# Value-gate products with the gate weights held still on column quarters, and three turns back

## The chip, the cores and the metric

The kernel runs on one core of one Trainium2 chip. The core has TensorE (PE, matrix products; the trace shows its weight loads apart, as PEld), VectorE (DVE), ScalarE (ACT), GpSimd (POOL) and SyncE (SP, which issues most transfers). The metric is the device time of one execution in microseconds, as the median of several runs; lower is better.

## The reference, cut to what matters

Windowed attention (8 batches, 8 heads, 576 tokens, 64 columns a head, window 128) feeds a mixture of 8 experts with two experts a token.

```
scores = scale * q @ k.T + bias, masked to 0 <= rel < 128      # per batch and head
attn   = softmax(scores)
x      = (attn @ v), heads side by side                        # 4608 x 512
logits = x @ w_gate;  noise_scale = log1p(exp(x @ w_noise))    # 4608 x 8 each
noisy  = logits + noise_scale * noise
top2 of noisy per token, softmax over the two
out[t] = sum over the two experts e: weight * relu(x[t] @ w1[e]) @ w2[e]
```

The gate logits are linear in x, and x is linear in v. So the kernel multiplies v by the gate weights first, a 16-column product for each head ("value gates"), appends these 16 columns to the head's 64 value columns, and gets its share of the logits out of the same product with the attention weights that gives x.

## The kernel before, in words

Work is cut into 32 pairs (a batch and two heads) of attention, then the experts' two products. A pair has five blocks of up to 128 queries. On PE a pair is: `scores` (L578, 18 products of 64x64 stationary tiles, in two bursts of 12 and 6), `trans` (L599, 13 transposes of the softmax tiles), and `weigh` (L616, 32 products of the turned weights with the values and their gate columns). DVE takes maxima (`top`), ACT exponentials (`soft`), and either of them evacuates PSUM (`evac`, L291 on ACT and L295 on DVE).

Every second pair starts a new value tile: 16 groups of value gates in all, one for a batch and four heads (`gates_of_values`). A group takes the transposed values `vt` (128 rows: two heads of 64 columns, twice, for 576 keys). For each of five blocks of keys and each of the two halves `c`, the keys' 128 (or 64) columns are loaded as the stationary operand and the 32 gate columns of `wgn` stream through (L516): 10 products, each shown by the trace as two records of PE, since a product of 32-bit numbers is done in two passes. The result has keys on partitions, and two copies (`gates_in`) put it beside the raw values `vraw`.

PSUM has eight banks: four for scores (two rings of two), one for the low half of `weigh`, and three in the ring `tb` that transposes, value gates, the high half of `weigh` and routing share.

After each batch its tokens are routed (logits, top two, a scatter of token numbers). Feed-forward work for experts 0 and 1 on the batches that are already routed (the first wave: L1306 first product, L1366 and L1371 second product) is woven into the end of attention; the second wave does all the rest and runs to the end.

The order of instructions on each engine is fixed before the run, by a small planner in the kernel (`Order`). It gives each piece of work a rank and an assumed duration, and plays the program with queues, buffers and transfers. The ranks come from a table of constants (`LOAD`, `STAGE`, `FFN0`, `HOLD` and others); `TURNED` is the assumed duration of a group of value gates on PE.

Of the kernel before, what the change touches and what calls it, by code (L numbers as in the profile page):

```python
# [8 lines left out]
F32 = mybir.dt.float32  # L9
# [10 lines left out]
B, H, S, D = 8, 8, 576, 64  # L20
N, DM, E, F = B * S, H * D, 8, 1024
W = 128
NQ = 5
# [18 lines left out]
BLOCKS = tuple(((DONE[-1], c - DONE[-1]),) if e < EARLY else ((0, 512), (512, 384), (896, c - 896)) for e, c in enumerate(CAPS))  # L42
HELD, MORE = 16, 8
LISTS = ((0, EARLY, DONE[-1], (CAP - DONE[-1] + 127) // 128), (EARLY, E, 0, (CAP + 127) // 128))
ZERO = 1340.8
LOAD = 885.97
VALUES = 252.36
GATE = (105.31, -144.49)
GATES = 473.91
ROUTE = -23.25  # L50
SCATTER = (-321.47, -1089.37, 1184.84)
FFN0, FFN1 = 144.02, 197.25
WEIGHTS = ((71.95, 139.15), (422.16, -43.96))
SEQUENCE = ((0, 0), (0, 1), (1, 0), (1, 1), (0, 2), (1, 2), (0, 3), (1, 3))
TOKENS = -282.53
STAGE = (793.51, 96.25, -887.0, -336.08, -38.4, -877.89, 219.3, -111.42)
MIDDLE = 339.64
RESULT = -1110.7
WEIGHTS_LATE = 521.8
SOON = -136.65  # L60
LISTED = (-1113.58, -714.36)
BIG, PARTS = 1899.33, 796.08
TIGHT = (1, 5, 7)
LATE = (-1193.61, -724.08, 210.07, 80.21, -368.28, 29.29, 453.02, -305.32, -534.88, -183.12, 1321.79, 251.28, 666.5, 311.48)
LAG = 0.2
SP_COST = 0.55
DMA_RATE = 360e3
DMA_LAG = 4.0
REST = 0.74
PACE = (36.32, -15.48)  # L70
HOLD = (-53.94, 64.86)
AHEAD = 301.5
GATHER_LAG, SCATTER_LAG, LISTED_LAG, TURN_LAG = 4.4, 5.0, 3.0, 4.0
STAY, TURN = -236.48, 0.13
TICK, WARM = 3.413, 1.28
WEIGH, TURNED = 2.2, 1.1

# [35 lines left out]
class Order:  # L115
# [48 lines left out]
    def put(self, ring, tile_):  # L164
        ring.free.append(tile_)
        self.serve(ring)
# [85 lines left out]
def attention_moe(ctx: ExitStack, tc: tile.TileContext, qk_, v, vt_, w_gate, w_noise, noise, w12,  # L252
                  out, xs, slots, eye):
    nc = tc.nc
# [10 lines left out]
    ap_ = att.enter_context(tc.tile_pool(name="att", bufs=1))  # L265
    order = Order()
    spawn, put, mark = order.spawn, order.put, order.set

    def ring(pool, count, shape, dtype, name):
        return Ring([pool.tile(shape, dtype, name=f"{name}{i}") for i in range(count)])  # L270

    def pe(us, rank, emit, join=True, shape=0):
        return Op((("PE", us, rank),), emit, join, shape)
# [10 lines left out]
    def either(a, b, rank, late, emit):  # L284
        return Op((("ACT", a, rank), ("DVE", b, rank + late)), emit)
# [3 lines left out]
    def copy(e, o, i, **kw):  # L289
        if e == "ACT":  # L290
            nc.scalar.activation(o, i, AF.Copy, **kw)  # L291
        elif kw:
            nc.vector.tensor_scalar(o, i, kw["scale"], None, op0=OP.mult)
        else:
            nc.vector.tensor_copy(o, i)  # L295
# [12 lines left out]
    denr = ring(ap_, 2, [128, 2, NQ, 2], F32, "den")  # L308
    xr = ring(ap_, 3, [128, NQ, 256], F32, "x")
    ltr = ring(ap_, 2, [128, NQ, H, 16], F32, "lt")  # L310
    gsr = ring(ap_, 1, [128, 128], F32, "gs")

    PAIRS = B * NP
    n = PAIRS * NQ
# [10 lines left out]
    ident = const.tile([128, 128], F32, name="ident")  # L325
# [7 lines left out]
    wgn = const.tile([128, 4, 32], F32, name="wgn")  # L333
# [25 lines left out]
    def masks():  # L359
# [10 lines left out]
        for g in range(NP):  # L370
            for h, odd in ((2 * g, 0), (2 * g + 1, 0), (2 * g, 1), (2 * g + 1, 1)):
                yield either(0.28, 0.17, -20 + 5 * g, LATE[9], lambda e, h=h, odd=odd: bias_of(e, h, odd))
            if not g:
# [4 lines left out]
    def set_ups():  # L378
# [41 lines left out]
        for z, (ap, r) in enumerate([(xs, N * XW)] + [(out, r * DM) for r in range(0, NPAD, 512)]):  # L420
            row_ = 4 * DM + (0 if z else rest_)
            yield from move(1e6, 16 + ZERO * z, lambda ap=ap, r=r, row_=row_: nc.sync.dma_start(
                dram(ap, r, [[row_, 128], [DM, 4], [1, DM]]), zero[:, None, :].to_broadcast([128, 4, DM])))
# [12 lines left out]
    def gate_weight(z, w, h, parts):  # L436
        yield from move(2e4, -LOAD + GATES, lambda: nc.sync.dma_start(
            wgn[h * D:h * D + D, :, h * 16 + z * E:h * 16 + z * E + E],
# [5 lines left out]
    sb, tb, ob, yb = Ring([bank[0:2], bank[5:7]]), Ring([*bank[2:4], bank[7]]), Ring([bank[4]]), Ring([])  # L444
# [9 lines left out]
    def loads():  # L454

        for k in range(PAIRS):
            rank = 5 * k - LOAD
            t = qks[k] = yield (qkr, rank)
# [17 lines left out]
    def all_values():  # L476
        for y in range(2 * B):
            rank = 10 * y - VALUES
            u = yield (vtr, rank)
# [22 lines left out]
    def gates_of_values(y, t, u, turned, landed):  # L502

        rank = 10 * y + GATE[0]
        spawn(ones_of(y, t, landed, rank))
        yield gated
        yield turned
        a = yield (tb, rank)
        c0 = y % 2 * 2

        def products():
            for i in range(NQ):
                r = min(S - 128 * i, 128)
                for c in range(2):
                    o = 64 * i + 32 * c
                    nc.tensor.matmul(a[0:r, o:o + 32], u[:, c, 128 * i:128 * i + r], wgn[:, c0 + c],  # L516
                                     start=i == c == 0, stop=False, skip_group_check=True)

        yield pe(TURNED, rank, products)
        put(vtr, u)  # L520
        yield landed
        done = Event(2)
        for z in range(2):
            spawn(gates_in(y, t, a, z, rank, done))
        yield done
        put(tb, a)

    def gates_in(y, t, a, z, rank, done):
        if z:
            to, from_ = t[0:64, 4, :, D:D + 16], a[0:64, 256:320].rearrange("p (h e) -> p h e", h=4)  # L530
        else:
            to, from_ = t[:, 0:4, :, D:D + 16], a[:, 0:256].rearrange("p (i h e) -> p i h e", i=4, h=4)
        yield either(*((0.11, 0.13) if z else (0.28, 0.34)), rank, LATE[2], lambda e: copy(e, to, from_))
        mark(done)
        mark(valued[y])
# [116 lines left out]
    def burst(k, group):  # L652
        r0 = k * NQ + group[0] + STAGE[0]
        if not k:
# [16 lines left out]
    def unit(k, i, group, s, topped):  # L671
        t = k * NQ + i
        r0, r1, r2, r3, r4, r5, r6, r7 = (t + z for z in STAGE)
        g, y = k % NP, k // 2
# [69 lines left out]
    def part(i, a, pt, r4, parted):  # L744

        half_ = i in (0, 4)
        yield either(0.28 if half_ else 0.39, 0.34 if half_ else 0.47, r4, LATE[3], lambda e: evac(e, i, a, pt))
        put(tb, a)
# [24 lines left out]
    def logits(b):  # L773


        yield written[b]
        rank = 20 * b + GATE[1]
        lt = lts[b]
# [18 lines left out]
    u = ap_.tile([128, NQ, E], F32, name="u")  # L797
# [16 lines left out]
    def route(b):  # L814
        yield gates[b]
        if b:
            yield routed[b - 1]
        rank = 20 * b - ROUTE
        V = nc.vector
# [155 lines left out]
        else:  # L975
            yield Op((("POOL", 1.55, rank), ("DVE", 0.8, rank + LATE[10])), lambda g: tables(engine[g], 2), slows=0.4)
        a = yield (tb, rank)
# [8 lines left out]

        rank = 20 * b + SCATTER[2 if b == B - 1 else b + 1 in CUTS]
        yield pool(1.08, rank, scatter)
# [148 lines left out]
    def early_rank(e, f):  # L1137
        return WEIGHTS[e][0] + WEIGHTS[e][1] * f if e < EARLY else 1000 + step_of(e) + f

# [23 lines left out]
    def weight(e, f, t, rank):  # L1163
# [18 lines left out]
        if e < EARLY:  # L1182
            yield either(1.35, 1.13, rank, LATE[12], largest)
        else:
# [23 lines left out]
    def split(e, f, z, t, parts, rank, both):  # L1208
# [11 lines left out]
        if e < EARLY:  # L1220
            yield Op((("POOL", 2.85, rank), ("DVE", 0.66, rank + WEIGHTS_LATE)), low, slows=0.6)
        else:
# [115 lines left out]
    def middle(blk, f, t, rank, end):  # L1338
# [11 lines left out]
        else:  # L1350
# [3 lines left out]
            blk.h[f][1].append(hl)  # L1354
        yield either(0.052 + c * 0.000833, 0.067 + c * 0.00104, rank - MIDDLE, LATE[8], lambda e: relu(
            e, hh[:, 0:c], t[:, 0:c]))
        yield dve(0.07 + c * 0.00104, rank - MIDDLE, lambda: nc.vector.scalar_tensor_tensor(  # L1357
            hl[:, 0:c], t[:, 0:c], 0.0, hh[:, 0:c], op0=OP.max, op1=OP.subtract))
# [24 lines left out]
    def downs_of(steps, ranks):  # L1383
        for (blk, f), rank in zip(steps, ranks):
# [24 lines left out]
            for piece in pieces_:  # L1409
                end = yield pe(0.655 * len(piece) + (0.1 if blk.cut is not None else 0.0), rank,  # L1410
                               lambda: [mm2(blk, f, j, r, ev[2]) for j, r in piece], False)
                if f == 7:
                    for j, r in piece:
                        spawn(result(blk, j, r, rank - RESULT, end))
            spawn(after(blk, f, ev[3] if blk.last else None, end))

    def last_downs(blk, rank):

        blk.y = []
        for j, r in blk.tiles:  # L1420
# [4 lines left out]
            for f in range(8):  # L1425
# [3 lines left out]
                end = yield pe(0.655, rank, lambda: mm2(blk, f, j, r, ev[2]), False)  # L1429
            spawn(result(blk, j, r, rank - RESULT, end))  # L1430
        to = yield (yor, rank)
# [95 lines left out]
    def first_tokens():  # L1527
        for e, blk in enumerate(first):
            yield from tokens(blk, ranks1[8 * e] - TOKENS)

# [84 lines left out]
    def second_ids():  # L1615
        yield order.now + LISTED_LAG
        for (e0, e1, s0, nt), (rows, t) in zip(LISTS, ids2):
            if e0:
                yield ranked
            rank = LISTED[e0 > 0]  # L1620
            yield from token_numbers(range(e0, e1), s0, nt, rows, t, rank)
# [22 lines left out]
    def second_tokens():  # L1644
        for q, blk in enumerate(second):
            yield from tokens(blk, 1000 + 8 * q - AHEAD if q else FFN1 - SOON)

# [32 lines left out]
    with ExitStack() as ob:  # L1680
# [4 lines left out]
        with tc.For_i(0, reach, 1) as j:  # L1685
            e = nc.values_load(tab[:, 0, bass.ds(j, 1)], engines=[mybir.EngineType.SP], min_val=0, max_val=E - 1)
            r = nc.values_load(tab[:, 1, bass.ds(j, 1)], engines=[mybir.EngineType.SP], min_val=0,
                               max_val=(E * EROWS - 128) // UNIT)
# [11 lines left out]
            t = op.tile([128, 4, 128], F32, name="ot")  # L1700
# [5 lines left out]
            for a in range(2):  # L1706
                h = op.tile([128, 4, 128], F32, name="oh")
# [10 lines left out]
            o = ow.tile([128, DM], F32, name="oo")  # L1718
# [47 lines left out]
```

## Time and profile before

| what | value |
|---|---|
| median of 3 runs | 1049.65 us (1047.02 to 1052.15) |
| the profiled execution: time | 1048.76 us |
| its span, first to last instruction | 1046.9 us |
| PE busy | 1022.2 us (98% of the span) |
| PE records of the value gates (L516) | 320, in 16 groups, from 16.4 to 224.4 us |
| mean granted TensorE clock | 0.995 |

The span lies 1.9 us under the execution's time, and that time 0.9 us under the median. Busy times of PE come from records that overlap: a record is longer than the time until the next one starts, so what a piece of work costs is read from start to start.

### The profile page before, as it was taken

To read this page: it belongs to the slowest core of one execution; us is meant where nothing else is said; L and a number is where in the kernel's file an instruction comes from. 1 tells how busy PE (TensorE), PEld (TensorE's weight loads), DVE (VectorE), ACT (ScalarE), POOL (GpSimd) and SP (SyncE) were. 2 spreads that over 40 slices of the span, in tenths; PEclk is the share of its full clock that TensorE was granted. 3 is DMA by queue.
4 is the path that set the end of the run, shared out by engine and by line. 5 is a ranking of instruction groups with operands and counts; after the bars stand their busy time and mean duration, and the time that the engine had idled before them with its cause. 6 is when DMAs were issued, how large, how long until landed. Compare 5 with 4: busy or idle time off the path is not lost.

```text
span 1046.9 us, 23487 instructions
## 1 busy us (share of the span) xinstructions
PE 1022.2 (98%) x8934; PEld 666.1 (64%) x8934; DVE 616.2 (59%) x2350; ACT 471.1 (45%) x1118; POOL 348.4 (33%) x458
## 2 busy tenths in 40 slices
PE   7999999999999999999999999999999999999997
PEld 6787778886666679654565457545744664564455
DVE  5988988977779981469836733663457241332111
ACT  5878776764422662225633433362326231332211
POOL 1085798124433531320433033312332330421103
PEclk9999999999999999999999999999999999999999
DMA  8989898963357971793768167805953471753113
GB/s 297 404 278 372 305 298 302 293 201 66 64 106 196 192 135 24 198 265 66 102 86 212 48 112 117 215 12 100 197 132 45 87 98 36 123 72 48 15 26 50
DMA packets 137123, 157.00 MB, mean 150 GB/s; under 512 B 90529, under 2 KB 100849, under 8 KB 137009
## 3 DMA queue, kind: packets, MB, share of 16 engines
q1 hardware_dynamic: 119488, 116.14, 39.4%
q0 software_dynamic: 17520, 39.34, 22.0%
q8 instruction: 71, 1.16, 0.5%
q14 instruction: 44, 0.35, 0.1%
HBM read 95.11 MB, written 40.91 MB: 130 GB/s over the span
## 4 chain that ended last, share of the span: by engine, by line
PE 90%; DVE 5%; ACT 2%; DMA 1%; issue 1%; POOL 1%; SPq 0%; DVEq 0%; ACTq 0%
PE bank L1306 35%; PE bank L1366 29%; PE bank L1371 6%; PE bank L616 6%; PE bank L599 5%; PE bank L578 4%; PE bank L516 3%; DVE held L1218 1%; PE bank L1479 1%; DVE p L584 1%; ACT pT L291 1%; PE bank L1447 1%; DVE ahl L1357 0%; POOL out_dram L1501 0%; DMA xs_dram<-x 0%
## 5 line engine op out<-in xcount | busy, mean ns | idle before, releaser
L1306 PEld LDWEIGHTS <-held 128*128 128x128 f16 x2424 | 234.2, 98 | 127.3 <-issue 2.9
L1306 PE MATMUL bank<-bx,held 128*128 128x512 f16 (+7 forms) x1752 | 301.9, 324 | 0.0
L1501 POOL DMA_INDIRECT out_dram<-yo,ix x62 | 99.8, 1609 | 429.8 <-ACT yo L291 393.9
L1357 DVE SCALAR_TENSOR_TENSOR bhl<-bank,bhh 128x384 f16<-128x384 f32 (+6 forms) x152 | 84.6, 557 | 265.5 <-ACT bhh L1334 265.4
L1334 ACT ACTIVATE bhh<-bank 128x512 f16<-128x512 f32 (+6 forms) x135 | 66.2, 490 | 323.9 <-PE bank L1306 319.0
L1366 PE MATMUL bank<-held,bhh 128*128 128x512 f16 x696 | 207.0, 379 | 0.0
L1366 PE MATMUL bank<-held,bhl 128*128 128x512 f16 x348 | 131.9, 379 | 0.0
L1366 PEld LDWEIGHTS <-bhh 128*128 128x128 f16 x768 | 74.8, 98 | 79.6
L592 ACT ACTIVATE p<-p,nm 128x192 f32<-128x192 f32 (+2 forms) x288 | 102.9, 427 | 7.4 <-DVE nm L584 7.1
L584 DVE CUSTOM_DVE_ANT_0 p<-bank,bias 128x192 f32<-128x192 f32 (+2 forms) x288 | 80.7, 327 | 7.2 <-PE bank L578 5.6
L1251 POOL DMA_INDIRECT xg<-xs_dram,ix x62 | 65.7, 1059 | 48.2 <-DVE bias L1606 10.5
L616 PE MATMUL bank<-vraw,pT 64*64 64x81 f32 (+1 forms) x2048 | 78.2, 242 | 0.2 <-ACT pT L291 0.2
L1306 PE MATMUL bank<-ax,held 128*128 128x256 f16 (+1 forms) x672 | 75.4, 266 | 1.8 <-DVE ahl L1357 1.7
L616 PEld LDWEIGHTS bank<-vraw,pT 64*64 64x64 f32 (+1 forms) x2048 | 69.7, 138 | 9.0 <-issue 3.3
L599 PE MATMUL bank<-ident,p 128*128 128x128 f32 x416 | 68.0, 291 | 4.9 <-DVE pT L295 3.3
L578 PE MATMUL bank<-qk 64*64 64x192 f32 (+2 forms) x1152 | 64.9, 328 | 6.0 <-DMA qk<-in_qk_dram 4.5
L291 ACT ACTIVATE pT<-bank 128x384 f32<-128x384 f32 (+1 forms) x106 | 45.0, 446 | 50.2 <-PE bank L599 50.1
L291 ACT ACTIVATE held<-held,wsc 128x512 f16<-128x512 f32 x88 | 59.6, 715 | 16.1 <-DVE wsc L1237 12.1
L1366 PEld LDWEIGHTS <-bhl 128*128 128x128 f16 x384 | 37.6, 98 | 45.3
L1218 DVE SCALAR_TENSOR_TENSOR held<-held,wsc,held 128x512 f16<-128x512 f32 x85 | 61.4, 765 | 0.0
L599 PEld LDWEIGHTS bank<-ident,p 128*128 128x128 f32 x416 | 45.7, 144 | 24.4 <-issue 6.9
L291 ACT ACTIVATE yo<-bank,gw 128x512 f32<-128x512 f32 (+3 forms) x70 | 46.5, 680 | 31.2 <-PE bank L1366 18.0
(244 smaller groups left out, 1466.7 us busy)
## 6 DMA issues: line engine op xcount, KB each, us to landing
held<-in_w_dram SPq DMA_DIRECT2D x60, 512.0 KB
qk<-in_qk_dram SPq DMA_DIRECT2D x31, 576.0 KB
vraw<-in_v_dram SPq DMA_DIRECT2D x16, 810.0 KB
out_dram<-xg SPq DMA_DIRECT2D x10, 1024.0 KB
vt<-in_vt_dram SPq DMA_DIRECT2D x16, 576.0 KB
xs_dram<-x SPq DMA_DIRECT2D x16, 320.0 KB
xs_dram<-x SPq DMA_DIRECT2D x16, 256.0 KB
spare<-in_w_dram SPq DMA_DIRECT2D x4, 512.0 KB
```

Of the source, the lines that this page charges most:

```text
L291: nc.scalar.activation(o, i, AF.Copy, **kw)
L578: nc.tensor.matmul(s[j % 2][half:half + 64, o:o + c], qk[rows, j * 64:j * 64 + 64], qk[rows, k1 - c:k1], start=True, stop=True)
L584: nc.vector.tensor_tensor_reduce(out=p[:, place(j):place(j) + c], in0=s[z][:, o:o + c], in1=bias4[:, g, z, 192 - c:192], scale=-0.125, sca ...
L592: nc.scalar.activation(pv, pv, AF.Exp, bias=nm[:, z:z + 1], scale=-1.0)
L599: nc.tensor.transpose(t[:, z * 128:z * 128 + 128], p[:, a * 128:a * 128 + 128], ident)
L616: nc.tensor.matmul(o[z * 64:z * 64 + 64, c:c + VC], pt[rows, slot, from_:from_ + 64], t[rows, block, hh], start=(o is first_, z) not in be ...
L1218: nc.vector.scalar_tensor_tensor(lo, t, sc, hi, op0=OP.mult, op1=OP.subtract)
L1306: nc.tensor.matmul(t[:, 0:blk.n], wp[:, c], blk.x[:, x + c, 0:blk.n], start=c == 0 and z == 0, stop=c == 3 and z == 2)
L1334: nc.scalar.activation(o, i, AF.Relu)
L1357: yield dve(0.07 + c * 0.00104, rank - MIDDLE, lambda: nc.vector.scalar_tensor_tensor(hl[:, 0:c], t[:, 0:c], 0.0, hh[:, 0:c], op0=OP.max, ...
L1366: nc.tensor.matmul(blk.y[j][0:r], h[:, cs], wp, start=f == 0 and m == 0, stop=f == 7 and m == 2)
L1501: ins = nc.gpsimd.indirect_dma_start(out=out, out_offset=bass.IndirectOffsetOnAxis(ap=blk.ix[0:r, j:j + 1], axis=0), in_=t[0:r], in_offset ...
```

## The change

A group's operands change places. The 32 gate columns of a half `c` are now the stationary operand, on a quarter of the array's columns, and 320 keys stream through: keys 0 to 319 for quarters 0 and 1, keys 256 to 575 for quarters 2 and 3 (so 64 keys are done twice, to give all products one shape). Four products take the place of ten. The result has gates on partitions, so it is copied to a new tile `gt` (128 x 320, one buffer) by ACT or DVE, the bank goes back to `tb`, a bank is asked for again, and three transposes turn it: two with 128 columns of `gt`, one with 64. The two copies into `vraw` stay, the second from other columns. The table of constants is new throughout, and the planner's prices for the group are now `GATED` 0.58 and `TURNED` 0.33.

```diff
-GATE = (105.31, -144.49)
-GATES = 473.91
+GATE = (60.38, -351.0)
+GATES = 116.58
...
-WEIGH, TURNED = 2.2, 1.1
+WEIGH, GATED, TURNED = 2.2, 0.58, 0.33
...
-    gsr = ring(ap_, 1, [128, 128], F32, "gs")
+    gtr, gsr = ring(ap_, 1, [128, 320], F32, "gt"), ring(ap_, 1, [128, 128], F32, "gs")
...
         def products():
-            for i in range(NQ):
-                r = min(S - 128 * i, 128)
+            for k in range(2):
                 for c in range(2):
-                    o = 64 * i + 32 * c
-                    nc.tensor.matmul(a[0:r, o:o + 32], u[:, c, 128 * i:128 * i + r], wgn[:, c0 + c],
-                                     start=i == c == 0, stop=False, skip_group_check=True)
-
-        yield pe(TURNED, rank, products)
+                    q = 64 * k + 32 * c
+                    nc.tensor.matmul(a[q:q + 32, 0:320], wgn[:, c0 + c], u[:, c, k * 256:k * 256 + 320], start=True, stop=True)
+
+        yield pe(GATED, rank, products, True, 3)
         put(vtr, u)
+        gt = yield (gtr, rank)
+        yield either(0.34, 0.4, rank, LATE[2], lambda e: copy(e, gt, a[:, 0:320]))
+        put(tb, a)
+        a = yield (tb, rank)
+
+        def turn():
+            for z in range(2):
+                nc.tensor.transpose(a[:, 0:256].rearrange("p (k z c) -> p k z c", k=2, z=2)[:, :, z], gt[:, z * 128:z * 128 + 128], ident)
+            nc.tensor.transpose(a[0:64, 256:384], gt[:, 256:320], ident)
+
+        yield pe(TURNED, rank, turn)
+        put(gtr, gt)
...
-            to, from_ = t[0:64, 4, :, D:D + 16], a[0:64, 256:320].rearrange("p (h e) -> p h e", h=4)
+            to, from_ = t[0:64, 4, :, D:D + 16], a[0:64, 320:384].rearrange("p (h e) -> p h e", h=4)
```

The order on PE around the first group before, between the transposes of the first pairs (`p` are softmax tiles, `qk` the scores' operands; a row counts products, each two records in the trace):

```order
L599 MATMUL bank_69<-ident,p_91 128x128 x2
L599 MATMUL bank_73<-ident,p_92 128x128 x2
L516 MATMUL bank_68<-wgn,vt_85 128x32 x8
L516 MATMUL bank_68<-wgn,vt_85 64x32 x2
L599 MATMUL bank_69<-ident,p_87 128x128 x3
L578 MATMUL bank_71<-qk_80 64x64 x2
```

And the same place now, up to the turns:

```order
L609 MATMUL bank_69<-ident,p_91 128x128 x2
L609 MATMUL bank_73<-ident,p_92 128x128 x2
L515 MATMUL bank_68<-vt_85,wgn 32x320 x4
L588 MATMUL bank_71<-qk_80 64x64 x2
...
L588 MATMUL bank_72<-qk_80 64x192 x2
L609 MATMUL bank_69<-ident,p_87 128x128 x3
L609 MATMUL bank_73<-ident,p_88 128x128 x3
L526 MATMUL bank_68<-ident,gt_108 128x2x64 x2
L527 MATMUL bank_68<-ident,gt_108 64x128
L588 MATMUL bank_66<-qk_80 64x192 x2
```

The ten products in one piece became four, then a burst of scores and six transposes, and then the three turns.

On ACT, the copy that the turns wait for stands between exponentials (L602) of the same pairs:

```order
L291 ACTIVATE pT_99<-bank_68 128x384
L602 ACTIVATE p_87<-p_87,nm_93 128x192 x2
L602 ACTIVATE p_88<-p_88,nm_94 128x192 x2
L291 ACTIVATE gt_108<-bank_68 128x320
L602 ACTIVATE p_89<-p_89,nm_95 128x192 x2
```

The row with `gt_108` is new; 13 of the 16 such copies stand on ACT and 3 on DVE.

The first step of the first wave on PE before, behind the last group's products (row L516) and the `weigh` (L616) of the pair that takes them:

```order
L516 MATMUL bank_68<-wgn,vt_86 64x32 x2
L616 MATMUL bank_73<-vraw_83,pT_100 64x81 x4
...
L599 MATMUL bank_69<-ident,p_88 128x128 x2
L599 MATMUL bank_68<-ident,p_87 128x128 x3
L1306 LDWEIGHTS spare_125
L1306 MATMUL bank_71<-ax_202,spare_125 128x256
```

And now:

```order
L527 MATMUL bank_73<-ident,gt_108 64x128
L626 MATMUL bank_69<-vraw_83,pT_100 64x81 x4
...
L626 MATMUL bank_69<-vraw_83,pT_100 64x81
L626 MATMUL bank_70<-vraw_83,pT_100 64x81 x3
L1316 LDWEIGHTS spare_126
L1316 MATMUL bank_71<-ax_203,spare_126 128x256
```

It moved forward: before, it stood behind the 16th group; now it stands behind the 13th, and three more groups and more of attention come after it, woven with feed-forward steps. Between the turn of the first wave's token numbers (L1024, L1034 now) and this first step there stood on PE 8 `weigh`, 144 scores products of 64x64 tiles, 104 transposes and 4 groups; now there stand 6 `weigh`, 90 scores products, 70 transposes, 3 groups of four products and 3 of turns. The number of scores, transposes, `weigh` and feed-forward products in the whole program is unchanged.

## Rows read from the trace of the kernel before

**Rows 1.** The page: busy time of the engines, and the chain that ended last.
```profile
PE 1022.2 (98%) x8934; PEld 666.1 (64%) x8934; DVE 616.2 (59%) x2350; ACT 471.1 (45%) x1118; POOL 348.4 (33%) x458
...
PE 90%; DVE 5%; ACT 2%; DMA 1%; issue 1%; POOL 1%; SPq 0%; DVEq 0%; ACTq 0%
PE bank L1306 35%; PE bank L1366 29%; PE bank L1371 6%; PE bank L616 6%; PE bank L599 5%; PE bank L578 4%; PE bank L516 3%; DVE held L1218 1%; PE bank L1479 1%; DVE p L584 1%; ACT pT L291 1%; PE bank L1447 1%; DVE ahl L1357 0%; POOL out_dram L1501 0%; DMA xs_dram<-x 0%
```
**Rows 2.** Stretches: length, busy time by engine, granted clock, DMA share, GB/s.
```profile
core 0: us, PE busy (x) PEld busy (x) DVE busy (x) ACT busy (x) POOL busy (x), PEclk, DMA share, GB/s
0.00:60.00 60.00, 53.05 (x802) 42.41 (x804) 45.17 (x244) 41.21 (x118) 8.96 (x39) 1.00 0.90 328
60.00:120.00 60.00, 57.49 (x984) 47.22 (x980) 53.18 (x264) 49.39 (x145) 44.19 (x47) 0.97 0.93 336
120.00:180.00 60.00, 56.87 (x972) 46.89 (x970) 51.69 (x273) 42.30 (x117) 54.16 (x64) 0.97 0.91 304
180.00:230.00 50.00, 50.00 (x876) 41.82 (x879) 41.94 (x239) 34.55 (x100) 10.08 (x27) 1.00 0.89 266
...
400.00:1047.00 647.00, 639.51 (x3789) 368.99 (x3787) 289.72 (x770) 228.45 (x451) 165.63 (x186) 1.00 0.53 100
```
**Rows 3.** What PE waited for: total us, times, longest.
```profile
PE bank L578 <- DMA qk<-in_qk_dram: 4.5, 2, 3.4
PE bank L599 <- DVE pT L295: 3.3, 2, 1.8
...
PE bank L599 <- ACT pT L291: 1.1, 3, 0.5
```
**Rows 4.** PE in order of time: a group of products and its neighbours.
```profile
16.40 2.22 PE L516 MATMUL bank<-wgn,vt 128*128 128x32 f32 x20
18.55 0.55 PE L599 MATMUL bank<-ident,p 128*128 128x128 f32 x3
19.03 1.10 PE L578 MATMUL bank<-qk 64*64 64x64 f32 x24
```
**Rows 5.** The products of all groups: duration ns min/median/max, first and last start.
```profile
L516 PE MATMUL bank<-wgn,vt x320: 195/276/297, 16.4 to 224.4; 128*128 128x32 f32 x128, 128*64 128x32 f32 x32
```
**Rows 6.** PE in order of time: scores of 64x64 tiles.
```profile
40.58 0.87 PE L578 MATMUL bank<-qk 64*64 64x192 f32 x12
41.38 0.88 PE L599 MATMUL bank<-ident,p 128*128 128x128 f32 x6
...
101.15 1.64 PE L578 MATMUL bank<-qk 64*64 64x192 f32 x36
102.72 0.55 PE L599 MATMUL bank<-ident,p 128*128 128x128 f32 x3
```
**Rows 7.** One weigh by shapes (20.86 to 23.14 us): busy us, mean ns.
```profile
L616 PE MATMUL bank<-vraw,pT 128*64 128x81 f32 x32 | 1.4, 237 | 0.0
L616 PE MATMUL bank<-vraw,pT 64*64 64x81 f32 x32 | 1.1, 238 | 0.0
```
**Rows 8.** Copies out of PSUM on ACT: busy us, mean ns, idle before.
```profile
L291 ACT ACTIVATE pT<-bank 128x384 f32<-128x384 f32 x65 | 30.8, 488 | 33.2 <-PE bank L599 33.1
...
L291 ACT ACTIVATE pT<-bank 128x256 f32<-128x256 f32 x41 | 15.5, 378 | 17.0 <-PE bank L599 17.0
```
**Rows 9.** Token numbers turned and the first wave's first step, on PE.
```profile
169.76 0.26 PE L1024 MATMUL bank<-ident,gs 4*128 4x4 f32 x1
...
227.34 1.47 PE L1306 MATMUL bank<-ax,spare 128*128 128x256 f16 x12
```
**Rows 10.** Next numbers turned (235 to 250 us), tokens' transfers (240 to 260).
```profile
L1024 PE MATMUL bank<-ident,gs x1: 219/219/219, 242.4 to 242.4; 4*128 4x4 f32 x1
...
L1297 SPq DMA_TRANSPOSE ax<-xt x2: 1231/1266/1301, 256.1 to 258.0; - x2
```

More of the change, by code (lines that the diff above doesn't have):

```diff
@@ L44 @@
 LISTS = ((0, EARLY, DONE[-1], (CAP - DONE[-1] + 127) // 128), (EARLY, E, 0, (CAP + 127) // 128))
-ZERO = 1340.8
-LOAD = 885.97
-VALUES = 252.36
-GATE = (105.31, -144.49)
-GATES = 473.91
[L50 to L53, printed above, removed]
-SEQUENCE = ((0, 0), (0, 1), (1, 0), (1, 1), (0, 2), (1, 2), (0, 3), (1, 3))
[L55 to L62, printed above, removed]
+ZERO = 1301.11
+LOAD = 1222.75
+VALUES = 288.45
+GATE = (60.38, -351.0)
+GATES = 116.58
+ROUTE = 17.85
+SCATTER = (0.87, -1290.0, 1234.91)
+FFN0, FFN1 = 153.27, 218.69
+WEIGHTS = ((175.1, 198.06), (365.03, 171.86))
+SEQUENCE = ((0, 0), (0, 1), (1, 0), (1, 1), (0, 2), (1, 2), (0, 3), (1, 3))
+TOKENS = -264.25
+STAGE = (496.81, 135.88, -1126.82, -870.69, -11.82, -730.64, 219.3, -104.61)
+MIDDLE = 920.83
+RESULT = -1285.17
+WEIGHTS_LATE = 826.01
+SOON = -143.0
+LISTED = (-761.65, -714.11)
+BIG, PARTS = 2137.12, 224.79
 TIGHT = (1, 5, 7)
-LATE = (-1193.61, -724.08, 210.07, 80.21, -368.28, 29.29, 453.02, -305.32, -534.88, -183.12, 1321.79, 251.28, 666.5, 311.48)
+LATE = (-1353.2, -570.37, 218.91, 24.19, 2.46, 17.48, 459.81, -192.39, -664.76, -121.21, 1351.79, 167.54, 664.61, 304.11)
 LAG = 0.2
@@ L68 @@
 DMA_LAG = 4.0
[L69 to L72, printed above, removed]
+REST = 0.87
+PACE = (41.1, -37.68)
+HOLD = (-39.57, 205.98)
+AHEAD = 468.47
 GATHER_LAG, SCATTER_LAG, LISTED_LAG, TURN_LAG = 4.4, 5.0, 3.0, 4.0
-STAY, TURN = -236.48, 0.13
+STAY, TURN = -268.86, 0.13
 TICK, WARM = 3.413, 1.28
-WEIGH, TURNED = 2.2, 1.1
+WEIGH, GATED, TURNED = 2.2, 0.58, 0.33
 def dram(ap, offset, dims):
```

## The prediction

> **What bounds the kernel now.** I read the page first. PE is busy for 1022.2 of 1046.9 us, and the chain that ended last runs on PE for 90% of the span; no line of another engine has over 1% of it [rows 1]. A chain that stays on one engine says: take work from that engine, and look at what else is then close to its limit. The table by stretches shows where the second part matters. From 400 us on PE is without gaps but for the tail, while DVE is busy for 289.7 of 647 us; nothing there touches this change. In the first 230 us, where attention is, PE is busy for 53.05, 57.49, 56.87 and 50.00 us of 60, 60, 60 and 50, but the others are not far behind: DVE has 192 of 230 us (83%, and 89% between 60 and 120 us), ACT 167 (73%), and the DMA engines' share is 0.89 to 0.93 at 266 to 336 GB/s [rows 2]. The waits of PE say that they have not bitten yet: 4.5 us for the first loads, then 3.3 us for DVE's and 1.1 us for ACT's evacuations of transposes are the largest in attention [rows 3].
>
> The value gates have 3% of the chain on their one line [rows 1]; that is what the change can take from.
>
> **What it removes.** A group starts at 16.40 us and the next work on PE at 18.55 us: 2.15 us for 20 records, 0.108 us each [rows 4]. With 16 groups [rows 5] that is 34.4 us, which fits the 3% of the chain.
>
> **What the new products cost.** Four products in two passes are eight records of 320 columns. What a column costs, and whether products on different parts of the array run side by side, is in the scores. A burst of 36 records (18 products on quarters of 64 rows by 64 columns, widths 64, 128 and seven times 192 for each of two heads) takes 1.57 us from start to start, a burst of 12 (six products of 192) takes 0.80 us [rows 6]. If four products run at a time, one round lasts as long as its widest: 2 x (128 + 4 x 192) = 1792 columns in the long burst, 2 x 2 x 192 = 768 in the short one. The difference, 1024 columns in 0.77 us, is 0.75 ns a column, and leaves 0.22 us in the short burst for coming in and going out. One after the other, the long burst would have 2 x 3072 columns and take 4.6 us; so four at a time is shown, for 64 rows each. Tiles of all 128 rows are shown on halves: 32 records of 81 columns would take 1.94 us singly and 0.97 us in pairs, and the trace has 1.4 us busy, the latency of the last one (about 0.2 us) included [rows 7]. Pairs, then. Four of 128 rows on column quarters are nowhere in this trace. Bounds: 640 columns x 0.75 = 0.48 us without any entry cost, 0.70 us with it, 1.18 us if only two run at a time, 2.14 us singly. I take 0.70 us: side by side is what both kinds of tiles do.
>
> **What the turns cost.** Three transposes take 0.48 us from start to start beside a change of tile shape [rows 4]. The third turn has 64 columns and changes the shape again; nothing here times a transpose of this kind apart. From 0.32 us (three of 0.108) to 0.70 (0.48 and one more entry of 0.22); I take 0.50.
>
> A group thus costs 1.20 instead of 2.15 us. 16 x 0.95 = 15.2 us less on PE; with the lower ends 16 x 1.35 = 21.6, with two at a time and the dearer turns 16 x 0.27 = 4.3.
>
> **What it adds elsewhere.** A copy of 128 x 320 lies between the ACT rows for 256 and 384 columns, 378 and 488 ns [rows 8]: about 0.43 us, 16 times, 7 us in all, 13 of them on ACT. ACT has 63 us idle in 230, so this costs nothing by itself. But the turns now wait for it, and behind them in PE's queue stands everything else. In 12 of 16 groups a `weigh` or more stands on PE between products and turns: 2.3 us (1.4 and 1.1 busy [rows 7], less an overlap of about 0.2), against 0.43 us of copy, about 0.25 us of the products' latency (the mean of such records [rows 5, 7]), and the exponentials ahead of the copy in ACT's queue. That covers it if ACT is not over 1.6 us late. From nothing to about 0.5 us a group (8 us); I take 1 us in all. The group now asks `tb` for a bank twice, for shorter holds each. If the ring runs short of banks, a group pays a copy's 0.43 us, 7 us in all; PE's waits for evacuations out of this ring were 4.4 us in the whole run [rows 3], so the ring has banks to spare, and I put nothing on it.
>
> **The new order.** Two things follow. First, PE's cover shrinks for the others: over the first 230 us it has some 14 us less to do, so the same 192 us of DVE, with the three copies, fill 90%. Where DVE was at 89%, from 60 to 120 us, PE stood idle for 2.5 us, where it was at 84%, from 180 to 230 us, not at all [rows 2]. At 2.5 us for each 60, the 216 us have 9 us of gaps, against 8 now without the first loads (2.5 in the first 60, then 2.5, 3.1 and 0). 1.5 us more with a share for ACT and the loads, and up to 6 if DVE queues build up. Second, the first wave starts earlier. From the turn of its numbers to its first step PE had 57.6 us of work [rows 9]; now the order leaves 6 `weigh` (13.7 us), 90 scores products (five bursts' worth of 1.57 [rows 6], 7.9), 70 transposes (11 at the 0.16 of [rows 4]) and 3 groups (3.6): 36 us. Numbers turned at 242.4 had their tokens' last transfer issued at 258.0, 15.6 us later [rows 10], and a landing still to come. So the 36 us hide it, and with no such cover a wait of 16 us would stand there once. I cost it at nothing. Expert 1's weights are read later, which lightens the DMA engines in attention's first part. Everything behind 400 us keeps its pieces.
>
> **Sum**, against the profiled execution's own 1048.76 us, 0.9 below the median: 1048.76 - 15.2 + 1 + 1.5 = 1036.1.
>
> **Rivals.**
> *Others become late* (chance 0.15). DVE at 90%, loads at a share of 0.9, ACT's copy in PE's way. For: every engine's margin shrinks together, and the granted clock was 0.97 in the two stretches from 60 to 180 us, part of them at 1.2 GHz instead of 2.4, and 1.00 in the next, which has no gap [rows 2] (the first 60 us have gaps at 1.00 too). Against: PE's waits are few [rows 3]. With 6 us for DVE's queue and 4 for the turns in place of 2.5: 1043.5.
> *Two at a time* (0.07): 16 x 0.47 = 7.5 us saved with turns at 0.50; 1043.8. For: only pairs are shown for 128 rows. Against: the scores' four.
> *Every change of tile shape empties the array* (0.04). A group would have four changes (into quarters and out, into the 64-column turn and out) where I charged some 0.36 us for all. At the 276 ns of a record [rows 5] each they are 1.10 us, 0.75 more, 12 us over the program: 1048. The short burst of scores had 0.22 us for two changes, which speaks against it. The Trainium skill states such a rule, in TensorEngine Tiling (Array Packing), Key Properties: "Changing tiling mode (not just tile) drains the TensorE"; the 0.22 us of this trace bounds what a drain can cost.
> *One at a time, slower than before* (0.05). If full-height quarters exclude each other, products cost 2.14 us and with the turns 2.64, 0.49 over the old group: 1048.76 + 7.8 + 2.5 = 1059. It turns into a loss once products take more than 1.65 us less the new waits, about 1.5. Against it are the pairs of [rows 7].
> *Better than forecast* (0.09): entry costs vanish and waits don't grow, 1027.
>
> **How the numbers follow.** The forecast, 1036, has 0.60, and its own range is 1030 to 1041. The range for all is 1028 to 1046: it takes in the late engines and the pairs, and leaves out the serial case, the drained array and the best end. Half a per cent, about what a measurement of this kernel can tell from no change, is 5.2 us. Below 1044.4 lie the forecast, the best case, most of the pairs (0.05) and half of the late engines (0.08): 0.82. Above 1054.9 lies the serial case with a little more: 0.06. The rest is 0.12.
>
> **What would show it.** In the changed kernel's profile: a group of products with 8 records, the next work starting about 0.70 us after its first (1.2 in pairs, over 2 singly); the turns' next work about 0.50 us after theirs; PE busy about 15 us less, near 1007; waits of PE on the `gt` copy near 1 us in total; DVE near 90% in the attention stage, PE's gaps there not much above 10 us; no wait at the first step of the first wave. The prediction is wrong if four products take over 1.2 us, if PE's idle time grows by over 6 us, or if the wave's first step waits for its tokens or weights.

## The result, and the profile after

The changed kernel takes 1040.55 us (median of 6 runs, 1039.17 to 1041.02) beside 1051.43 us for the kernel before: ratio 0.9905, 95% interval 0.9886 to 0.9924. The ratio is not the quotient of the two medians (0.9897): it is taken from all runs but the slow ones, which leaves out one of 1987.04 us of the kernel before. In another round of runs it had 0.9904 (0.9882 to 0.9926). The forecast was 1036, range 1028 to 1046.

The page of the changed kernel, as [rows 1] (line numbers are 10 higher behind the value gates):

```profile
span 1037.4 us, 23210 instructions
...
PE 1006.1 (97%) x8790; PEld 635.8 (61%) x8790; DVE 623.1 (60%) x2359; ACT 476.4 (46%) x1130; POOL 330.2 (32%) x442
...
PE 83%; DVE 9%; DMA 3%; ACT 2%; issue 2%; POOL 1%; SPq 0%; ACTq 0%; POOLq 0%; DVEq 0%
```

PE is busy for 16.1 us less, but the span fell by 9.5 us only. What PE is idle, span less busy, rose from 24.7 to 31.3 us. The chain says the same: DVE's share of it went from 5% to 9%, PE's from 90% to 83%.

A group of products, and a `weigh` and the turns behind it, in order of time, as [rows 4]:

```profile
35.51 0.75 PE L515 MATMUL bank<-vt,wgn 128*32 128x320 f32 x8
36.18 2.35 PE L626 MATMUL bank<-vraw,pT 128*64 128x81 f32 x64
38.46 0.44 PE L526 MATMUL bank<-ident,gt 128*128 128x128 f32 x2
38.73 0.27 PE L527 MATMUL bank<-ident,gt 128*64 128x128 f32 x1
38.84 0.49 PE L609 MATMUL bank<-ident,p 128*128 128x128 f32 x3
```

Eight records take 0.67 us from their start to the next work's start, and the three turns 0.38 us: 1.05 us in place of 2.15 for this group. Over the 16 groups the products take the same, and the turns 0.42 us on average without idle time: 0.33 to 0.38 where more transposes follow, 0.42 to 0.46 ahead of scores, 0.48 to 0.50 ahead of a `weigh`. The four full-height quarters run side by side; singly they would need 2.14 us, by the prediction's estimate.

The stretches, with the columns of [rows 2]:

```profile
0.00:60.00 60.00, 50.74 (x815) 36.63 (x816) 47.87 (x253) 47.20 (x135) 13.52 (x43) 1.00 0.94 344
60.00:120.00 60.00, 56.98 (x1033) 42.86 (x1028) 55.64 (x300) 47.02 (x133) 42.54 (x55) 1.00 0.99 338
120.00:180.00 60.00, 56.13 (x979) 40.69 (x973) 51.48 (x304) 41.33 (x121) 15.03 (x39) 1.00 0.94 313
180.00:230.00 50.00, 48.66 (x684) 35.61 (x684) 42.40 (x219) 32.96 (x97) 17.36 (x36) 1.00 0.79 245
...
400.00:1037.00 637.00, 629.20 (x3662) 358.13 (x3659) 288.89 (x767) 221.14 (x439) 164.03 (x182) 1.00 0.53 101
```

In the first 230 us PE is now idle for 17.5 us where it was 12.6. DVE is busy for 197 of 230 us (86%, and 93% from 60 to 120 us). The clock, 0.97 from 60 to 180 us before, is 1.00.

The longest waits of PE, as [rows 3]:

```profile
PE bank L588 <- DMA qk<-in_qk_dram: 5.5, 3, 3.4
PE bank L609 <- DVE pT L295: 5.0, 6, 1.4
PE bank L609 <- ACT pT L291: 3.2, 3, 1.7
...
PE bank L609 <- ACT gt L291: 0.8, 2, 0.5
```

The waits for evacuations of transposes grew from 4.4 to 8.2 us; the wait for the new copy is small.

To see where the time went, I added up for all records of PE the time from a record's start to the next one's, with the idle time apart. (The page's idle time is 11 us more than that between records: it takes in some 3.4 us ahead of PE's first record and 7.4 to 7.8 us behind its last.) Between the profiled executions the end of PE's work moved by -9.9 us:

```
                               before    after   difference
products (and turns)            34.62    17.51      -17.11
weigh                           75.30    72.42       -2.88
scores and transposes          122.14   124.71       +2.57
idle between records            13.93    20.10       +6.17
all the rest                                         +1.4
```

Of the -2.88 us of `weigh`, 2.6 are the clock: before, two of them fell into stretches at 1.2 GHz and took 3.37 and 3.80 us in place of 2.28. From the kernel before's chain that ended last and from its stretches of 10 us:

```profile
89.01 3.37 PE bank L616 x63
...
80.00:90.00 10.00, 7.97 (x140) 6.38 (x141) 9.12 (x45) 8.28 (x25) 9.47 (x10) 0.90 1.03 400
90.00:100.00 10.00, 10.00 (x180) 8.27 (x176) 8.30 (x47) 9.42 (x31) 1.62 (x3) 0.93 1.04 399
...
160.00:170.00 10.00, 9.53 (x146) 8.21 (x142) 7.93 (x46) 6.79 (x18) 9.30 (x12) 0.83 0.92 333
```

The clock stands in the ratio too. Over the rounds that give each run's mean granted clock, the kernel before took 1046.5 us in its 19 runs at 0.997 and 1051.2 in its 15 at 0.992. The changed kernel had 0.995 to 0.998. Where both had the same mean clock, it gains 6.2 us (0.997), 7.4 (0.996) and 8.2 (0.995), with 2 to 4 runs of the changed kernel at each. So some 2 to 4 of the 10 us go with a better clock; whether the change itself brings that was not tried.

### The profile page after: what moved, and what is told of

Read it like the earlier page. It is cut to its first block, busy times and chain, and to the rows that moved or that the text cites. A ratio compares the mean times of both kernels' runs of the same rounds, so it can differ in the third digit from the quotient of the medians.

```text
span 1037.4 us, 23210 instructions
## 1 busy us (share of the span) xinstructions
PE 1006.1 (97%) x8790; PEld 635.8 (61%) x8790; DVE 623.1 (60%) x2359; ACT 476.4 (46%) x1130; POOL 330.2 (32%) x442
## 4 chain that ended last, share of the span: by engine, by line
PE 83%; DVE 9%; DMA 3%; ACT 2%; issue 2%; POOL 1%; SPq 0%; ACTq 0%; POOLq 0%; DVEq 0%
PE bank L1316 34%; PE bank L1376 28%; PE bank L1381 6%; PE bank L626 5%; PE bank L588 3%; PE bank L609 3%; DMA held<-in_w_dram 2%; DVE p L594 1%; DVE held L1228 1%; DVE xt L1299 1%; DVE pT L295 1%; PE bank L1489 1%; DMA qk<-in_qk_dram 1%; DVE x L738 1%; PE bank L515 1%
## 5 line engine op out<-in xcount | busy, mean ns | idle before, releaser
L602 ACT ACTIVATE p<-p,nm 128x192 f32<-128x192 f32 (+2 forms) x288 | 103.3, 427 | 14.6 <-DVE nm L594 14.3
L609 PE MATMUL bank<-ident,p 128*128 128x128 f32 x416 | 70.4, 288 | 10.4 <-DVE pT L295 5.0
L626 PE MATMUL bank<-vraw,pT 64*64 64x81 f32 (+1 forms) x2048 | 75.5, 237 | 2.0 <-DVE nm L594 0.7
L1261 POOL DMA_INDIRECT xg<-xs_dram,ix x62 | 65.4, 1054 | 32.9 <-issue 10.4
L626 PEld LDWEIGHTS bank<-vraw,pT 64*64 64x64 f32 (+1 forms) x2048 | 67.1, 135 | 13.7 <-issue 3.1
L291 ACT ACTIVATE held<-held,wsc 128x512 f16<-128x512 f32 x95 | 64.1, 714 | 11.6 <-DVE wsc L1247 4.2
L1228 DVE SCALAR_TENSOR_TENSOR held<-held,wsc,held 128x512 f16<-128x512 f32 x92 | 68.9, 790 | 0.0
L1186 DVE TENSOR_REDUCE wam<-held 128x2 f32<-128x1024 f32 x48 | 57.6, 1211 | 13.3 <-DMA held<-in_w_dram 13.2
L291 ACT ACTIVATE yo<-bank,gw 128x512 f32<-128x512 f32 (+2 forms) x75 | 49.7, 678 | 30.9 <-PE bank L1376 17.0
```

What stands on the lines that cost most here:

```text
L602: nc.scalar.activation(pv, pv, AF.Exp, bias=nm[:, z:z + 1], scale=-1.0)
L609: nc.tensor.transpose(t[:, z * 128:z * 128 + 128], p[:, a * 128:a * 128 + 128], ident)
L626: nc.tensor.matmul(o[z * 64:z * 64 + 64, c:c + VC], pt[rows, slot, from_:from_ + 64], t[rows, block, hh], start=(o is first_, z) not in be ...
L1228: nc.vector.scalar_tensor_tensor(lo, t, sc, hi, op0=OP.mult, op1=OP.subtract)
```

## The experiments

Beside each run stands its ratio to the kernel before of the same chip, since that kernel's own median went from 1047.6 to 1050.4 us between chips. 0.001 of ratio is 1.05 us. "Idle" is span less PE busy on the run's page: 24.7 us before, 31.3 us after. The expectations count the idle time between PE's records instead, as the table above does: 13.9 us before, 20.1 after. That count is given as "between records".

**The changed kernel once more**, as the mark of its round.

> The changed kernel itself, as the mark for the other runs of this chip: 1040 to 1041 us. Its profiled execution was 1039.17 us with 0.998 of the full clock; others had 0.995 to 0.997, so this one may be a little longer.

1039.29 us, ratio 0.9904. Its page has 1039.5 us of span and 1005.1 of PE busy: idle 34.4 us, 22.9 between records. Two executions of one kernel thus differ by 3 us of idle time. This one waited 4.1 us for a later transfer of tokens, up to 373.9 us, and 2.0 for `vt`, and had two stretches at half clock ahead of its tail, where the other had none. Its scores and transposes take 122.3 us, as in the kernel before: the +2.57 us of the table are not there.

**Slower products, same order.**

```diff
-            for k in range(2):
-                for c in range(2):
+            twice = ((0, 0), (0, 1), (1, 0), (1, 1)) * 2
+            for k, c in twice:
```

> The changed kernel in its own order, but each group does its four products two times into the same bank (8 products, 16 records); the result stays. PE gets 16 times about 0.54 us more, 8.6 us. Theory 1 (the products are shorter, so PE runs ahead of DVE and ACT, and part of the gain goes into waits for their evacuations): the time rises by only 3 to 6 us over the changed kernel, and PE's waits fall by 3 to 5 us. Rival A (the waits come from where the new order puts its pieces, whatever the products take): it rises by the full 8 to 9 us, and the waits stay near 20 us.

1044.46 us, ratio 0.9968 (0.9953 to 0.9982): 6.7 us over the changed kernel by the ratios, 5.2 by the medians. PE busy 1012.1, idle 31.7 us, 20.6 between records, within what two executions of the changed kernel differ by. The added products take 9.1 to 9.7 us by PE's records. Neither expectation is met clearly: between a half and three quarters of the added work shows in the time, the waits stay as rival A has them, and it does not tell theory 1 from rival A.

**Without the copy into `gt`.**

```diff
-        yield either(0.34, 0.4, rank, LATE[2], lambda e: copy(e, gt, a[:, 0:320]))
+        yield either(0.34, 0.4, rank, LATE[2], lambda e: None)
...
+    nc.gpsimd.memset(gtr.free[0], 0.0)
```

> The changed kernel in its own order, but the 16 copies into gt are left out; gt is set to zero once, so the value gates are zero and routing goes by the noise alone. The turns wait for nothing. Theory 1 (DVE and ACT as a whole are late): taking 7 us from ACT and DVE gives back 1 to 3 us. Rival B (the chain products, copy, turns holds PE and the banks): nearly all of the 6 us of added waits go, the time falls by 5 to 7 us. Rival A: under 1 us, since only 0.8 us of PE's waits name this copy.

1037.02 us, ratio 0.9891 (0.9870 to 0.9913), 1.4 us less by ratios; idle 33.2 us, 21.9 between records. Its interval overlaps the changed kernel's. The copy is not what holds PE: rival B's 5 to 7 us are not there.

**The code alone, with the old table.** The block of constants from `ZERO` to `TICK, WARM` is that of the kernel before.

> The changed code with the table of constants of the kernel before (the prices of the group, 0.58 and 0.33, stay new): the products alone, without the new order. Theory 1: the same gain in PE's work, the same or more waits, 1038 to 1043 us. Rival A (the new table brought the waits): 1033 to 1036. Rival C (the new table is what keeps the gain): over 1044.

1052.43 us, ratio 1.0057 (1.0033 to 1.0081): slower than before. Its page and its longest waits:

```profile
PE 1007.4 (96%) x8790; PEld 637.1 (61%) x8790; DVE 617.9 (59%) x2346; ACT 480.6 (46%) x1144; POOL 348.8 (33%) x457
...
PE bank L609 <- ACT pT L291: 7.5, 13, 1.2
PE bank L588 <- DVE nm L594: 4.7, 4, 1.5
...
PE bank L609 <- DVE pT L295: 3.5, 7, 1.0
PE bank L626 <- DVE lt L738: 2.3, 1, 2.3
```

PE's work is down by 15 us, nearly as in the changed kernel, and its idle time is 43.1 us (32.1 between records), 18 more than before. The whole gain went into waits, spread over many small ones. Theory 1 and rival A both miss; rival C holds. It is slower than the kernel before at a like clock too: 1052.3 us beside 1049.1 at 0.995. The changed kernel has 1040.9 there. The stretches of attention:

```profile
0.00:60.00 60.00, 50.89 (x830) 36.70 (x834) 48.41 (x263) 47.92 (x136) 14.36 (x43) 1.00 0.91 335
60.00:120.00 60.00, 53.17 (x892) 40.12 (x881) 51.78 (x244) 49.84 (x143) 41.69 (x44) 0.94 0.95 345
120.00:180.00 60.00, 51.43 (x948) 38.28 (x948) 51.05 (x279) 44.38 (x124) 50.91 (x64) 1.00 0.91 306
180.00:230.00 50.00, 47.86 (x733) 34.67 (x729) 40.90 (x231) 33.35 (x97) 9.86 (x25) 1.00 0.83 244
```

DVE is busy for 192 of these 230 us, less than the 197 of the changed kernel, and yet PE idles for 26.7 us where that idles for 17.5. So DVE's share alone does not tell PE's waits.

**Is that PE running ahead?** The same with each group's products three times.

```diff
+            thrice = ((0, 0), (0, 1), (1, 0), (1, 1)) * 3
+            for k, c in thrice:
```

> The changed code with the old table, in its own order, each group's four products done three times into the same bank (the result stays): 24 records in place of 8, 17 to 19 us more work on PE in 16 groups, so that a group takes about as long as the old one. Theory 1 (waits are given back as PE gets slower): PE's idle time falls from 32 us to about 15, and the time stays within 4 us of the 1052 us without the repeats. Rival B (the copy and the second bank make the waits): the waits stay, and the time is 1069 us.

1065.27 us, ratio 1.0156 (1.0132 to 1.0180). PE busy rose by 19.3 us, idle fell from 43.1 to 35.7 us (from 32.1 to 24.5 between records), and the time rose by 10.4 us by the ratios, 12.8 by the medians. So some 40% of the slowing comes back from waits: theory 1 has a part, not the whole, and neither of its two figures, nor rival B's. With a group as long as the old one (1.75 us of products and 0.42 of turns) PE still idles 11 us more than before.

**Or the copy, in that order?** The same edit as in the run without the copy, on the old table.

> The changed code with the old table, in its own order, without the 16 copies into gt (gt is zero, routing goes by the noise). Theory 1: a few us, 2 to 5, since ACT and DVE get 7 us of work less. Rival B: the idle time falls from 32 us to below 18 and the time by 12 us or more, to 1040 or less.

1053.54 us, ratio 1.0038 (1.0021 to 1.0056), idle 41.9 us (30.8 between records). The time is 2.0 us less by the ratios, the lower end of theory 1's figure, but the intervals overlap. Rival B falls here too.

**The order alone: old products, new table.**

> The old products with the new table (the old group's price of 1.1 stays): the order without the products. Theory 1 and C (the new table feeds PE better, the old products hide that): PE's idle time at or below the 14 us of before, time 1045 to 1051. Rival A (the new order itself brings waits): idle near 20 us, 1054 to 1058.

1072.48 us, ratio 1.0223 (1.0192 to 1.0254), slower than every other kernel of the study, and over rival A's figure too. Some of its stretches:

```profile
60.00:120.00 60.00, 54.41 (x928) 44.62 (x919) 48.91 (x241) 39.08 (x107) 49.38 (x57) 0.97 0.87 294
...
180.00:230.00 50.00, 47.96 (x632) 36.46 (x631) 36.25 (x197) 23.02 (x66) 19.19 (x39) 1.00 0.71 241
230.00:300.00 70.00, 62.78 (x777) 46.45 (x781) 59.54 (x258) 42.84 (x114) 41.34 (x53) 0.93 0.53 121
```

Idle 38.2 us (27.3 between records), and the clock is under 1.00 in several stretches (mean 0.989, and 0.984 to 0.989 in all its runs). PE is busy for 8.7 us more than before with the same work, so the 23 us are not idle time alone. DVE is busy for 73% from 180 to 230 us, so PE's 2 us of gaps there are not a full DVE. No expectation is met. Here, too, the planner's price of a group, 1.1, is far from the 2.15 us measured, as it is in the kernel before.

**The prices as measured.** The new table, with 0.67 us for the products and 0.42, the mean over the groups, for the turns as the planner's prices.

```diff
-WEIGH, GATED, TURNED = 2.2, 0.58, 0.33
+WEIGH, GATED, TURNED = 2.2, 0.67, 0.42
```

> The changed code with the new table, but the planner's prices of the group as measured, 0.67 for the products and 0.42 for the turns in place of 0.58 and 0.33; this makes another order from the same ranks. If right prices make a better order: 1033 to 1037. Theory O (a table holds only for the durations with which it was made): 1042 to 1060.

1054.00 us, ratio 1.0043 (1.0026 to 1.0060). The pieces of work are the same; what differs, by 0.09 us in two prices, is the order, and which of ACT and DVE makes some of the copies. The idle time is 43.4 us (32.2 between records). Right prices with this table make a worse order, 14.6 us worse by the ratios, 13 to 14 at a like clock of 0.995 and 0.996.

**Is it one full engine?** Three reliefs. First DVE: the 64 DVE products that write the logits' tile (15 us in all by their records) are left out.

```diff
-            yield dve(0.2 if c == 3 else 0.17, r7, lambda: times(o, i, c, lt, D, D + 16))
+            yield dve(0.2 if c == 3 else 0.17, r7, lambda: None)
...
+    for t in ltr.free:
+        nc.gpsimd.memset(t, 0.0)
```

> The changed kernel in its own order, without the 64 DVE products that write the logits' tile lt (15 us of DVE in the attention stage; lt is zero, so routing goes by the noise). Theory D (DVE's share of the attention stage, 89% and more, is what PE waits for in the end): PE's idle time falls from 20 to 23 us to 15 or less, time 1031 to 1035 beside 1039.3. Theory O (an order fits one set of durations; waits come from single places where queues don't mesh, not from one full engine): idle stays over 18 us, time 1037 to 1040.

1037.37 us, ratio 0.9886 (0.9861 to 0.9912), idle 29.0 us, 18.1 between records: 1.9 us less by the ratios, with intervals that overlap. The relief was smaller than planned: records of DVE overlap, and its busy time fell by 7.6 us only (623.1 to 615.5). Theory D's times (1031 to 1035) and its idle time (15) are not there; theory O's time is, and its idle time barely. The same on the old table:

> The changed code with the old table, in its own order, also without the 64 DVE products into lt. Theory D: the 32 us of idle time fall to 22 or less and the time by 10 us or more, to 1042 or less. Theory O: the time stays at 1048 or more.

1046.62 us, ratio 0.9977 (0.9957 to 0.9998), 8.4 us less by the ratios, 6.2 at a like clock (0.995); idle 38.1 us, 27.2 between records, 5 us less, while DVE's busy time fell by 10.7 us. Here DVE has up to half of the lost time; neither theory D's 1042 nor theory O's 1048 is met. Then the DMA engines: no transfers that fill the output with zeros (the output's sums are left without a start).

```diff
-            yield from move(1e6, 16 + ZERO * z, lambda ap=ap, r=r, row_=row_: nc.sync.dma_start(
+            yield from move(1e6, 16 + ZERO * z, lambda ap=ap, r=r, row_=row_: z or nc.sync.dma_start(
```

> The changed kernel in its own order, without the ten transfers that fill the output with zeros (10 of some 70 MB that the DMA engines move in the first 230 us). If the DMA share near 1.0 between 60 and 180 us delays loads on which PE waits: time 1033 to 1036. If the loads are early enough: 1038 to 1040.

```profile
60.00:120.00 60.00, 57.33 (x1030) 43.19 (x1030) 56.09 (x302) 47.75 (x136) 42.20 (x55) 1.00 0.76 241
120.00:180.00 60.00, 56.26 (x973) 40.69 (x972) 51.57 (x304) 40.57 (x119) 15.05 (x39) 1.00 0.77 239
```

1040.85 us, ratio 0.9910 (0.9884 to 0.9937). The DMA share fell from 0.99 and 0.94 to 0.76 and 0.77, and PE's busy time in these stretches, 57.33 and 56.26 us, is that of the changed kernel within 0.4 us. The time is just over the 1038 to 1040 of loads that are early enough. A share near 1.0 did not hold PE here.

**A turn of full width.** The third turn with 128 columns.

```diff
-            nc.tensor.transpose(a[0:64, 256:384], gt[:, 256:320], ident)
+            nc.tensor.transpose(a[:, 256:384], gt[:, 192:320], ident)
...
-            to, from_ = t[0:64, 4, :, D:D + 16], a[0:64, 320:384].rearrange("p (h e) -> p h e", h=4)
+            to, from_ = t[0:64, 4, :, D:D + 16], a[64:128, 320:384].rearrange("p (h e) -> p h e", h=4)
```

> The changed kernel in its own order, but the third turn takes 128 columns of gt (192 to 319) in place of 64, and the second copy reads partitions 64 to 127 of the bank; the result stays. If a change of tile shape costs PE 0.1 us or so on each side, the 16 groups give back 1 to 2.5 us and PE's three turns take 0.33 us in place of 0.42; if it costs nothing, the time stays within 0.5 us of the changed kernel.

1039.06 us, ratio 0.9908 (0.9884 to 0.9932), the same as the changed kernel. PE in order of time:

```profile
39.57 0.44 PE L526 MATMUL bank<-ident,gt 128*128 128x128 f32 x2
39.84 0.27 PE L527 MATMUL bank<-ident,gt 128*128 128x128 f32 x1
39.95 0.27 PE L609 MATMUL bank<-ident,p 128*128 128x128 f32 x1
```

The three turns take 0.38 us here and 0.42 over all groups either way, so the change of shape inside them costs nothing that shows.

No kernel that does the whole computation beat the changed one by more than its interval.

## Why the prediction was right, and where not

**Products.** Forecast 0.70 us a group by the scores' side-by-side rule, measured 0.67. The rivals of pairs (1.18) and of one at a time (2.14) fall with that one number.

**Turns.** Forecast 0.50 with an allowance for the 64-column turn, measured 0.42 on average; the wide turn shows that the allowance was for nothing. This is the term that was too dear: the group saves 1.07 us by the records, 17.1 us in all, where the sum had 15.2.

**The drained array.** The rival that every change of tile shape empties the array made a group 0.75 us dearer. The group is cheaper than my sum. What can be the cost of such a change is small: the turns take 0.04 to 0.08 us more ahead of scores, and some 0.1 more ahead of a `weigh`, than ahead of transposes. That a drain makes this difference was not tried. The Trainium skill states the rule without a price, in TensorEngine Tiling (Array Packing), Key Properties: a change of the tiling mode drains TensorE. The trace neither shows a drain nor rules out one of this size. The 2.57 us more of scores and transposes are no such cost, since the second execution of the same kernel does not have them.

**The copy.** Forecast 1 us of waits; PE's waits on `gt` are 0.8 us, and leaving the copies out gave 1.4 us with overlapping intervals. The size fits, though the second figure is not clear of the noise.

**The first wave's start.** Forecast no wait. The step starts as the `weigh` ahead of it is through, without idle time, here and in the second execution (175.66 us):

```profile
174.77 2.35 PE L626 MATMUL bank<-vraw,pT 128*64 128x81 f32 x64
177.05 1.48 PE L1316 MATMUL bank<-ax,spare 128*128 128x256 f16 x12
```

**The new order.** This is the step that was mis-sized. I put 1.5 us on it, from DVE's share and the gaps at that share. PE's idle time rose by 6.6 us on the page, 6.2 by its records, against 2.5 for both waits in the sum; in the second execution it rose by 9.7. That is over the 6 us which the prediction gave as a sign of being wrong, and that sign stands: the forecast of the time held, this step of it did not. DVE's share is 86% of the first 230 us, where the forecast had 90% of 216, and 93% in the fullest stretch. And it is the wrong measure: the old table under the new code has more idle time at a smaller share, and 8 us of DVE's time less gave 1.9 us. The reading of [rows 3] was also too kind: a wait of 1.5 us for DVE's maxima (`nm`) stands between the 3.3 and the 1.1 us that the prediction calls the largest.

**Luck in the total.** Between the two profiles PE's work ended 9.9 us earlier, where the sum had 12.7, by parts that pull both ways. The products gave 1.9 us more than the sum had, and the waits took 3.7 more. The clock gave back 2.6, for which the sum had no term. Scores, transposes and all the rest took 4.0 more, and the cause of that stays open. At a like clock the gain is 6 to 8 us.

**What the forecast did not see** is how much the order itself was worth. The sum has no term for it but PE's cover and the first wave's place. In fact neither half of the change gains alone: the code with the old table is at 1.0057, the table with the old code at 1.0223, and both together at 0.9905. The same PE work ran with 31 to 43 us of idle time, by the order. So the 1% is not "the products less some waits" but a saving of 17 us on PE that is lost whole under the old table. The new table is worth some 16 us to the new code by the ratios (1.0057 to 0.9904), 11 at a like clock. My sum came near because it assumed, without a row for it, what the new table then did: an order about as tight as the old one.

**What stays open.** Which feature of an order makes its idle time. PE running ahead explains some 40% of the old table's added idle time, DVE's load up to half of its lost time (these two may be the same waits), the copy nothing clear of the noise; the transfers that fill the output, left out under the new table, nothing measurable. The rest are waits of 0.2 to 2.3 us in many places. That an order only fits the durations it was found with agrees with all three mismatched orders, but no run shows why at a single place. A rival was not tried: the two tables of before and after may be picked ones, and any order that is not picked may lose 10 us or more, whatever durations it was made for. A small change of a price in the kernel before would tell.

## What to carry to other kernels

Where PE has nearly no gaps, a piece's saving can be read off its records from start to start, and products on separate column quarters could here be priced from other tiles that the trace shows side by side (0.70 us forecast, 0.67 measured). Whether the saving reaches the end depends on the order: run the new code with the old table and the old code with the new one, before the whole difference is put down to either. Do not take an engine's busy share for the price of its lateness: take some of its work away and see, and check by how much its busy time really fell. Compare runs at a like granted clock where the difference is only 1%.

## What was not expected of the hardware

In the kernel before, a gap of 1.8 us on PE [rows 3], the longest there for DVE, ended at 87.6 us and stood ahead of a stretch with a granted 1.2 GHz; the changed kernel has a gap of 1.35 us ahead of 158.46 us, behind which the clock stayed at 2.4 GHz. That is no rule about gaps: the other such stretch before, from 166.5 us, has no gap over 0.47 us in the 15 us ahead of it. The first line is the kernel before's, the others are the changed kernel's:

```profile
87.61 1.40 PE L599 MATMUL bank<-ident,p 128*128 128x128 f32 x6 [1.78 <-DVE pT L295]
...
156.34 0.77 PE L609 MATMUL bank<-ident,p 128*128 128x128 f32 x5
158.46 0.44 PE L609 MATMUL bank<-ident,p 128*128 128x128 f32 x2 [1.35 <-DVE pT L295]
158.82 0.75 PE L515 MATMUL bank<-vt,wgn 128*32 128x320 f32 x8
```

Such stretches came and went between executions of one kernel (mean clock 0.998 in one, 0.995 in another, of the changed kernel), and each lengthened the work in it: 3.37 and 3.80 us for a `weigh` that takes 2.28 elsewhere. A difference of 2 or 3 us between two profiles is within that.

A weight load of 32 columns is hardly shorter than one of 64 (106 and 110 ns). The eight loads of a group, two for each tile, would take 0.85 us one behind the other; in the group at 35.5 us they lie within 0.16 us, so they too run side by side:

```profile
35.50 0.16 PEld L515 LDWEIGHTS bank<-vt,wgn 128*32 128x32 f32 x8 [0.17 <-DVE nm L594]
...
L515 PEld LDWEIGHTS bank<-vt,wgn x128: 106/106/109, 15.0 to 232.8; 128*32 128x32 f32 x128
...
L527 PEld LDWEIGHTS bank<-ident,gt x16: 110/110/112, 17.6 to 248.7; 128*64 128x64 f32 x16
```
